# The last mixer of a gated attention and gMLP kernel, in pairs of row tiles with seven block products for eight

## The chip, the cores and the metric

The kernel runs on one core of a Trainium2 chip. The metric is the device time of one execution in microseconds (us). Three executions of the kernel before the change took 705.53, 705.56 and 706.84 us; their median is 705.56 us.

The engines are named as the profile names them: PE is the matrix engine (PEld its weight loads), DVE the Vector engine, ACT the Scalar engine, POOL GpSimd, SP the engine that issues most DMA transfers. PSUM is the memory that matmuls write, eight banks of 512 float32 columns for each of 128 partitions.

## The reference

One sequence of S = 2048 rows and D = 1024 columns goes through two branches, and a gate per row mixes them:

```python
g = _sigmoid((x * gate_w).sum(-1, keepdims=True))
a = _A_ref(x, A_wqkv, A_wo)          # attention over 8 positions, 2 apart, 32 heads of 32; then @ wo
b = _B_ref(x, B_w_in, B_w_sp, B_b_sp, B_w_out)
return g * a + (1 - g) * b
```

and the second branch is

```python
z = _gelu(jnp.einsum('bsd,df->bsf', x, w_in))        # f = 2 * 1792
z1 = z[..., :Fh].copy()
z2 = _layernorm(z[..., Fh:], axis=-1)
g = jnp.einsum('ts,bsf->btf', w_sp, z2) + b_sp[None, :, None]
return jnp.einsum('bsf,fd->bsd', z1 * g, w_out)      # u = z1 * g, 2048 x 1792, times w_out, 1792 x 1024
```

The last line is what this document calls the mixer: u times `w_out`.

## The kernel before

The rows are cut into 16 row tiles of 128, the 1792 features into 14 tiles of 128. Stages follow each other on PE: the gates' and `z2`'s matmuls, the queries, keys and values, `z1`, then the spatial product and the mixer, in four chunks of four row tiles (512 rows). Attention itself runs on DVE beside the first stages and leaves its output in DRAM (`o_d`), from where `load_oT` brings it back transposed, one row tile at a time.

Chunks 0 and 1 of the spatial product are plain (`g_chunk`): each of the 14 feature tiles sums 16 products. Chunks 2 and 3 together are done by `seven_products(n)`, called seven times, each for the feature tiles n and n + 7: the product of a 2x2 block matrix with a 2x2 block matrix, in seven block products of eight matmuls where eight block products would be plain. The sums of blocks that this takes (`s_sum` for `z2`, `t_sums` for `w_sp`) are made on DVE in float16; to keep float16 in range the rows of `w_sp` are scaled up by powers of two beforehand (`scale_rows`) and `omg` (1 - g) for rows 8 to 15 is scaled back down (`row_powers_back`). Partial sums that serve two results are copied on ACT from one PSUM bank to another, and matmuls go on adding there. `g_out` adds the bias and multiplies by `z1`, which an SP transfer has put in place; the result u lies in the first half of the `z2` tile of the feature before (`u_late`). While step n runs, DVE makes the sums of step n + 1.

`final_chunk(c)` then finishes four row tiles. For each half of 512 columns, `attn_mm` multiplies the attention output by `wo` (8 matmuls), `mixer_mm` multiplies u by `w_out` (14 matmuls), and `combine` scales the one by g on ACT, then the other by 1 - g on DVE, adding both; a transfer stores the row. The last row tile is cut into 512, 384 and 128 columns. The order is chunk 0, chunk 1, the seven steps, chunk 2, chunk 3.

Every engine runs its instructions in the order of the program text; nothing reorders them (`manual_schedule`). Work put off to a later moment goes through `beat`: `beat.at(t, f)` calls f once the matmuls written so far add up to time t, so that its instructions come at that point of the order. PSUM tiles come from one pool of eight banks in turn. SP's transfers are issued in program order as well, each when its own waits are over.

Of the kernel before, what the change touches and what calls it, by code (L numbers as in the profile page):

```python
# [27 lines left out]
FH = 1792  # L28
NF = FH // P
# [26 lines left out]
def kernel(  # L56
# [24 lines left out]
    def reg(off, n):  # L81
        return arena[:, off:off + n]
# [5 lines left out]
    o_d = dpool.tile([S, D], BF, name="o_d")  # L88
# [3 lines left out]
    ones = nc.const_aps.tensor(1.0, [P, 512], BF)  # L92
# [6 lines left out]
    ident = sm.tile([P, P], BF, name="ident")  # L99
# [36 lines left out]
    z2 = reg(Z_OFF, 16 * FH).rearrange("p (f i q) -> p f i q", f=NF, i=16)  # L136
    xT = reg(X_OFF, KT * S).rearrange("p (k s) -> p k s", k=KT)
    xT_flat = reg(X_OFF, KT * S)
    w_out_sb = reg(X_OFF, NF * D).rearrange("p (f n) -> p f n", f=NF)
# [23 lines left out]
    abs_out = reg(CD_OFF + 18944, 512)  # L163
# [3 lines left out]
    def half16(off, n):  # L167
        return reg(off, n * 512).bitcast(F16).rearrange("p (k t) -> p k t", k=n)
# [3 lines left out]
    u_first = reg(EF_OFF + 10240, 2048).rearrange("p (h i q) -> p h i q", h=2, i=8)  # L172
    t1 = half16(CD_OFF + 8192, 8)
    t2 = half16(A_OFF + 16384, 8)
    t3 = half16(EF_OFF, 8)
    t4_parts = [half16(X_OFF + NF * D, 4), half16(CD_OFF + 12288, 4)]

    x_v = x2.rearrange("(i q) d -> q i d", q=P)
    wq_v = A_wqkv.rearrange("(k p) c -> p k c", p=P)
# [5 lines left out]
    sync = nc.sync  # L185
# [38 lines left out]
    beat = Beat()  # L224
# [72 lines left out]
    TT = nc.vector.tensor_tensor  # L297
# [101 lines left out]
    def load_oT(a):  # L399
        sync.dma_start_transpose(oT_slots[a % 3], o_d[a * P:(a + 1) * P, :])  # L400
# [72 lines left out]
    for ch in range(NCH):  # L473
# [35 lines left out]
    for f in range(NF):  # L509
# [121 lines left out]
    def s_sum(n, k):  # L631
        a11, a12 = z2[:, n, 0:8, :], z2[:, n, 8:16, :]
        a21, a22 = z2[:, n + 7, 0:8, :], z2[:, n + 7, 8:16, :]
        if k == 0:
            TT(sums[0], a21, a22, ALU.add)
        elif k == 1:
            TT(sums[1], sums[0], a11, ALU.subtract)
        elif k == 2:
            TT(sums[2], a11, a21, ALU.subtract)
        else:  # L640
            TT(sums[3], a12, sums[1], ALU.subtract)

    def bank():
        return psum.tile([P, 512], F32, name="ps", tag="ps")

    def product(dst, lhs, rhs, first):
        for k in range(8):
            nc.tensor.matmul(dst[:], lhs[:, k, :], rhs(k), start=first and k == 0, stop=k == 7, skip_group_check=not first)  # L648

    def g_out(f, c, gsb):  # L650
        TT(gsb, gsb, bsp_bc[:, 512 * c:512 * (c + 1)], ALU.add)
        dst = u_late(f)[:, 4 * (c - 2):4 * (c - 1), :]
        TT(dst, gsb.rearrange("p (a q) -> p a q", a=4), dst, ALU.mult)

    def next_gsb():
        gs[0] += 1
        return gsb_slots[gs[0] % 3]

    def seven_products(n):
        fa, fb = n, n + 7  # L660
        for f in (fa, fb):
            sync.dma_start(u_late(f).rearrange("p (c a) q -> p c (a q)", c=2),
                           z1_d[2:4, :, f * 512:(f + 1) * 512].rearrange("c p t -> p c t"))
        more = n + 1 < 7
        e5 = asb_slots[n % 2]
        pa = bank()
        product(pa, z2[:, fa, 0:8, :], lambda k: b_lo[:, k], True)
        pb = bank()
        nc.scalar.copy(pb[:], pa[:])
        pe = bank()  # L670
        product(pe, sums[0], lambda k: t1[:, k], True)
        nc.scalar.copy(e5, pe[:])
        if more:
            s_sum(n + 1, 0)
        product(pb, sums[1], lambda k: t2[:, k], False)
        pc = bank()
        nc.scalar.copy(pc[:], pb[:])
        product(pa, z2[:, fa, 8:16, :], lambda k: b_lo[:, 8 + k], False)
        gsb = next_gsb()
        nc.scalar.copy(gsb, pa[:])  # L680
        g_out(fa, 2, gsb)
        product(pb, sums[2], lambda k: t3[:, k], False)
        gsb = next_gsb()
        TT(gsb, pb[:], e5, ALU.add)
        g_out(fb, 3, gsb)
        product(pc, sums[3], lambda k: b_hi[:, 8 + k], False)
        if more:
            s_sum(n + 1, 2)
        gsb = next_gsb()
        TT(gsb, pc[:], e5, ALU.add)  # L690
        g_out(fa, 3, gsb)
        product(pb, z2[:, fb, 8:16, :], lambda k: t4_parts[k // 4][:, k % 4], False)
        if more:
            s_sum(n + 1, 1)
            s_sum(n + 1, 3)
        gsb = next_gsb()
        nc.scalar.copy(gsb, pb[:])
        g_out(fb, 2, gsb)
        beat.run(56 * 512)

    def scaled_rows():
        t = beat.now
        natural(1)
        natural(2)
        for r in range(3):
            row_sums_fast(r)
        row_powers(0, 3, 1)
        row_powers_back()
        for r in range(4):
            load_wsp(3, r)  # L710
        for r in range(3):
            beat.at(t + 2.5 + 2.5 * r, lambda r=r: scale_rows(r))
        beat.at(t + 9.0, scaled_biases)
        for k, r in enumerate((3, 0, 1, 2)):
            beat.at(t + 8.0 + 3.5 * k, lambda r=r: load_wsp(2, r))

    def final_chunk(c):
        first = {}
        if c == 0:
            for a in range(3):  # L720
                for n0 in (0, 512):
                    first[a, n0] = mixer_mm(a, n0, 512)
            beat.flush(1e9)
            scaled_rows()
        if c == 1:
            for k in range(5):
                beat.at(beat.now + 12.0 + 3.0 * k, lambda k=k: t_sums(k))
            for k in range(2):
                beat.at(beat.now + 28.0 + k, lambda k=k: s_sum(0, k))
        for a in range(4 * c, 4 * c + 4):  # L730
            ob = ob_slots[a % 3]
            if a > 0 and a + 2 < 16:
                load_oT(a + 2)
            last = a == 15
            for part, (n0, nw) in enumerate(((0, 512), (512, 384), (896, 128)) if last else ((0, 512), (512, 512))):
                psa = attn_mm(a, n0, nw)
                psb = first[a, n0] if (a, n0) in first else mixer_mm(a, n0, nw)
                combine(a, n0, nw, part % 2, psa, psb)
                if last:
                    sync.dma_start(out2[a * P:(a + 1) * P, n0:n0 + nw], ob[:, n0:n0 + nw])  # L740
            if not last:
                sync.dma_start(out2[a * P:(a + 1) * P, :], ob)
# [14 lines left out]
    beat.at(t_rows + 40.0, lambda: natural(0))  # L757
    g_chunk(1)
    final_chunk(0)
    final_chunk(1)  # L760
    beat.flush(1e9)
    for k in (2, 3):
        s_sum(0, k)
    for n in range(7):
        seven_products(n)
    final_chunk(2)
    final_chunk(3)


# [28 lines left out]
```

## Time and profile before

The profiled execution took 706.58 us, of which the profile's span is 704.8 us; the median of the three timed executions is 705.56 us.

| stage | from, us | length, us | PE busy, us | DVE busy, us | ACT busy, us |
|---|---|---|---|---|---|
| `final_chunk(0)` | 463.0 | 39.8 | 38.30 | 14.84 | 11.68 |
| `final_chunk(1)` | 502.8 | 38.0 | 37.79 | 15.98 | 5.50 |
| seven steps | 540.8 | 84.6 | 84.23 | 48.98 | 19.70 |
| `final_chunk(2)` and `(3)` | 625.4 | 76.2 | 75.85 | 12.79 | 11.84 |
| whole execution | 0 | 704.8 | 696.2 | 458.3 | 279.1 |

In the lines of the profile, L561 is line 561 of the kernel. A group of instructions is given as line, engine, operation, output and input by name and shape, count, then busy time and mean duration in ns, then the engine's idle time just before them and what ended it. A line of the timeline starts with the time at which the instruction began and its duration. A window's columns are its ends and length, then busy time and count for PE, PEld, DVE, ACT and POOL, the granted PE clock, the DMA engines' busy share and GB/s. The chain that ended last is followed back from the last instruction, at each step to what released it.

### The profile page before, as it was taken

The numbers are of one execution on the slowest core, as the hardware profiler recorded it, in microseconds if no ns is written. First come the engines' busy times: TensorE is split into PE (matmuls) and PEld (weight loads), VectorE is DVE, ScalarE is ACT, GpSimd is POOL, SyncE is SP. The second block draws the span as 40 slices with busy tenths as digits, with TensorE's granted clock in tenths as the row PEclk, the third lists the DMA queues.
The fourth block names the chain that finished last, engine by engine and source line by source line (L and its number), as shares of the span: only waits on it lengthen the run. The fifth ranks groups of instructions, "written<-read, shape, count | busy, mean of one in ns | idle before, by whom it ended". The sixth has DMA issues, their size and how long they took to land.

```text
span 704.8 us, 8427 instructions
## 1 busy us (share of the span) xinstructions
PE 696.2 (99%) x3270; PEld 359.6 (51%) x3319; DVE 458.3 (65%) x496; ACT 279.1 (40%) x508; POOL 14.0 (2%) x23
## 2 busy tenths in 40 slices
PE   9999999999999999999999999999999999999998
PEld 4466666666665554444444444444444444444444
DVE  0000498999999999999999999852263565631111
ACT  4444544435369887344341229524211222221111
POOL 1000000000000211000000000000000000000000
PEclk9999999999999999999999999999999999999999
DMA  8994974976564122995249972299933111202210
GB/s 224 179 198 92 260 182 123 226 183 168 143 177 151 57 101 51 204 306 168 90 153 237 383 234 79 94 288 231 204 94 86 52 49 41 46 0 60 60 45 31
DMA packets 182967, 101.29 MB, mean 144 GB/s; under 512 B 145808, under 2 KB 171408, under 8 KB 182672
## 3 DMA queue, kind: packets, MB, share of 16 engines
q1 hardware_dynamic: 180624, 92.37, 50.1%
q10 hardware_dynamic: 2304, 8.39, 3.3%
q8 instruction: 26, 0.43, 0.2%
q14 instruction: 13, 0.11, 0.1%
HBM read 51.91 MB, written 32.57 MB: 120 GB/s over the span
## 4 chain that ended last, share of the span: by engine, by line
PE 97%; DMA 1%; issue 0%; SPq 0%; DVE 0%; DVEq 0%
PE ps L481 24%; PE ps L532 14%; PE psb L561 14%; PE ps L518 14%; PE ps L259 13%; PE ps L648 12%; PE psa L545 7%; DMA arena<-in_B_w_in_dram 1%; DMA arena<-o_d 1%; SPq L439 0%; SPq L437 0%; SPq L441 0%; DVE arena L569 0%; PE pt L584 0%; DVEq L569 0%
## 5 line engine op out<-in xcount | busy, mean ns | idle before, releaser
L481 PE MATMUL ps<-arena 128*128 128x512 bf16 x768 | 165.9, 379 | 0.0
L481 PEld LDWEIGHTS <-arena 128*128 128x128 bf16 x768 | 110.7, 144 | 55.1 <-issue 0.2
L303 DVE TENSOR_TENSOR arena<-arena 128x8192 bf16<-128x8192 bf16 x16 | 70.8, 4423 | 51.1 <-DMA arena<-k_d 50.9
L561 PE MATMUL psb<-arena 128*128 128x512 bf16 (+2 forms) x453 | 100.7, 372 | 0.5
L259 PE MATMUL ps<-arena 128*128 128x512 bf16 (+1 forms) x501 | 97.6, 353 | 1.3 <-DMA arena<-in_B_w_in_dram 0.6
L532 PE MATMUL ps<-arena 128*128 128x512 bf16 x439 | 96.6, 379 | 0.5
L518 PE MATMUL ps<-arena 128*128 128x512 bf16 x439 | 96.4, 379 | 0.5
L484 ACT CAST arena<-ps 128x512 bf16<-128x512 f32 x96 | 55.8, 587 | 93.2 <-PE ps L481 88.7
L569 DVE SCALAR_TENSOR_TENSOR arena<-psb,omg,arena 128x512 bf16<-128x512 f32 (+2 forms) x33 | 24.1, 734 | 104.9 <-PE psb L561 80.2
L648 PE MATMUL ps<-arena 128*128 128x512 f16 (+1 forms) x385 | 84.4, 379 | 0.4
L306 DVE TENSOR_TENSOR arena<-arena 128x4096 bf16<-128x4096 bf16 (+1 forms) x64 | 77.5, 1211 | 1.9
L259 PEld LDWEIGHTS <-arena 128*128 128x128 bf16 x512 | 50.2, 98 | 48.4 <-issue 1.9
L561 PEld LDWEIGHTS <-arena 128*128 128x128 bf16 x462 | 44.6, 98 | 52.1
L336 DVE TENSOR_TENSOR arena<-arena,att_A 128x8192 bf16<-128x8192 bf16 x16 | 70.7, 4421 | 0.2
L518 PEld LDWEIGHTS <-arena 128*128 128x128 bf16 x448 | 43.8, 98 | 52.7
L532 PEld LDWEIGHTS <-arena 128*128 128x128 bf16 x448 | 43.8, 98 | 52.6
L568 ACT ACTIVATE arena<-psa,g_s 128x512 f32<-128x512 f32 (+2 forms) x33 | 22.1, 674 | 121.9 <-PE psa L545 116.4
L648 PEld LDWEIGHTS <-arena 128*128 128x128 bf16 (+1 forms) x392 | 38.3, 98 | 46.3
L545 PE MATMUL psa<-arena 128*128 128x512 bf16 (+2 forms) x260 | 59.5, 372 | 1.6 <-DMA arena<-o_d 1.3
L520 ACT ACTIVATE arena<-ps 128x512 bf16<-128x512 f32 x56 | 32.2, 597 | 51.5 <-PE ps L518 39.1
L264 ACT ACTIVATE arena<-ps 128x512 bf16<-128x512 f32 (+1 forms) x64 | 34.3, 539 | 25.5 <-PE ps L259 25.3
L545 PEld LDWEIGHTS <-arena 128*128 128x128 bf16 x264 | 25.5, 98 | 31.2 <-DMA arena<-o_d 1.5
(93 smaller groups left out, 399.7 us busy)
## 6 DMA issues: line engine op xcount, KB each, us to landing
arena<-k_d SPq DMA_DIRECT2D x8, 960.0 KB, 7.3
arena<-v_d SPq DMA_DIRECT2D x8, 960.0 KB, 5.4
z_d<-arena SPq DMA_DIRECT2D x14, 512.0 KB, 4.0
arena<-in_A_wqkv_dram SPq DMA_DIRECT2D x24, 256.0 KB, 4.5
arena<-in_B_w_in_dram SPq DMA_DIRECT2D x4, 1024.0 KB, 6.6
q_d<-arena SPq DMA_DIRECT2D x32, 128.0 KB, 2.3
k_d<-arena SPq DMA_DIRECT2D x32, 128.0 KB, 2.3
v_d<-arena SPq DMA_DIRECT2D x32, 128.0 KB, 2.5
```

What stands on the lines that cost most here:

```text
L259: nc.tensor.matmul(ps[:, 0:N], xT[:, kt, i * P:(i + 1) * P], w2[:, kt, ZC * c:ZC * c + N], start=(kt == 0), stop=(kt == KT - 1))
L264: nc.scalar.activation(z2[:, 4 * c:4 * c + n // P, i, :], ps[:, 0:n].rearrange("p (f q) -> p f q", q=P), ACT.Gelu_apprx_tanh, accum_out=s1 ...
L303: TT(prod.rearrange("p (w j c) -> p w j c", w=W, j=8, c=C), in0, in1, ALU.mult)
L306: return lambda: TT(pv[:, :, 0:half], pv[:, :, 0:half], pv[:, :, half:2 * half], ALU.add)
L336: TT(prod.rearrange("p (w j d h) -> p w j d h", w=W, j=8, d=DH, h=HG), in0, in1, ALU.mult)
L481: nc.tensor.matmul(ps[:].rearrange("p (t c) -> p t c", t=4), lhsT, wgt[:, :, kt, :], start=(kt == 0), stop=(kt == KT - 1))
L484: nc.scalar.copy(st[:, j % 4, :], ps[:])
L518: nc.tensor.matmul(ps[:], w1[:, kt, (f % 4) * P:(f % 4 + 1) * P], xT[:, kt, 512 * c:512 * (c + 1)], start=(kt == 0), stop=(kt == KT - 1))
L532: nc.tensor.matmul(ps[:], z2[:, f, i, :], wsp[:, i, :, :].rearrange("p a t -> p (a t)"), start=(i == 0), stop=(i == 15))
L545: nc.tensor.matmul(psa[:, 0:nw], oT_slots[a % 3][:, kt, :], wo_sb[:, kt, n0:n0 + nw], start=(kt == 0), stop=(kt == KT - 1))
L561: nc.tensor.matmul(psb[:, 0:nw], u_tile(f, a), w_out_sb[:, f, n0:n0 + nw], start=(f == 0), stop=(f == NF - 1))
L648: nc.tensor.matmul(dst[:], lhs[:, k, :], rhs(k), start=first and k == 0, stop=k == 7, skip_group_check=not first)
```

## The change

The mixer of row tiles 8 to 15 (chunks 2 and 3) is no longer `mixer_mm`. Row tiles are taken in four pairs, the 14 feature tiles in two halves of seven and `w_out` in two halves of columns, so that u of a pair is a 2x2 block matrix and `w_out` another; `late_mix` multiplies them with the same scheme as the seven steps, seven block products of seven matmuls each. The attention's products stay as they are, 16 matmuls per row tile.

- `w_largest` (four reductions over `w_out`) and `whole_power` find one power of two for `w_out`; `whole_power` takes the largest of 128 partitions by a transpose on PE, a reduction on DVE and a matmul with ones that spreads it again, and multiplies `omg` by what scales back. Both are placed in `final_chunk(1)` through `beat`.
- In step n of the seven, for n of 1 and more, `w_scale(n - 1)` scales two tiles of `w_out` in place and `w_sum` makes four float16 sums of its halves, in the second halves of the `z2` tiles that the step before has used. `u_sums(n - 1)` on ACT adds up absolute values of u, from which `whole_power` later takes the power for u.
- After the seven steps, `late_chunks` does the attention products of row tiles 8 to 11 (`attn_pair`, `attn_half`) with the last tile's weights, the power for u and the first pair's sums (`prepare`: `u_scale`, then four `u_sum`) beside them; then pair 0, the attention products of row tiles 12 and 13, pairs 1, 2 and 3, and last the attention products of 14 and 15, with the last row tile cut as before. `prepare(q + 1)` stands after the sixth product of pair q.
- In the pairs ACT copies partial sums between banks and DVE combines; for the last pair ACT also scales the mixer's part.
- The transposed loads of row tiles 10 to 15 (`late_oT`) move: 10 ahead of the seven steps, 11 to 14 to their end, 15 once row 8's attention product frees its place. Two copies on ACT bring `u_first` into `z2`.

The diff, cut to its core:

```diff
@@ seven_products
         gsb = next_gsb()
         nc.scalar.copy(gsb, pa[:])
+        if n:
+            u_sums(n - 1)
         g_out(fa, 2, gsb)
+        if n:
+            w_scale(n - 1)
         product(pb, sums[2], lambda k: t3[:, k], False)
...
         g_out(fb, 3, gsb)
+        if n:
+            w_sum(n - 1, 0)
+            w_sum(n - 1, 1)
         product(pc, sums[3], lambda k: b_hi[:, 8 + k], False)
...
         g_out(fa, 3, gsb)
+        if n:
+            w_sum(n - 1, 2)
+            w_sum(n - 1, 3)
         product(pb, z2[:, fb, 8:16, :], lambda k: t4_parts[k // 4][:, k % 4], False)
...
+    def whole_power(src, up1):
+        v = nc.vector
+        v.tensor_scalar(top[:], src, TINY, None, ALU.max)
...
+        v.tensor_copy(top_b[:], top_i[:].bitcast(F32))
+        yield
+        po = psum.tile([P, 512], F32, name="po", tag="ps")
+        pt = po[0:1, 0:P // 2].bitcast(BF)
+        nc.tensor.transpose(pt, top_b[:], ident[:])
+        v.tensor_reduce(top_1[:], pt, AX.X, ALU.max)
+        yield
+        nc.tensor.matmul(po[:], ones[0:1, 0:P], top_1[:].to_broadcast([1, 512]), start=True, stop=True)
+        v.tensor_copy(top[:], po[:, 0:1])
...
+        v.tensor_scalar(omg[:, 8:16], omg[:, 8:16], back[:].bitcast(F32), None, ALU.mult)
+        yield
...
+    def w_scale(j):
+        for f in ((j + 1) % 7, (j + 1) % 7 + 7):
+            nc.vector.tensor_scalar(w_out_sb[:, f, :], w_out_sb[:, f, :], w_up[:].bitcast(F32), None, ALU.mult)
...
+    def u_scale(q):
+        v = z2[:, :, 2 * q:2 * q + 2, :]
+        nc.vector.tensor_scalar(v, v, u_up[:].bitcast(F32), None, ALU.mult)
...
+    def late_mix(q, done, added, ready):
+        s = late_sums[q % 2]
+        a, b = 8 + 2 * q, 9 + 2 * q
+        e5 = late_e5[q % 2]
+        pa = bank()
+        product7(pa, lambda j: z2[:, j, 2 * q, :], lambda j: w_tiles(j)[0], True)
+        pb = bank()
+        nc.scalar.copy(pb[:], pa[:])
+        pe = bank()
+        product7(pe, lambda j: s[0][:, j, :], lambda j: w_t(j, 0), True)
+        added(pe, e5)
+        product7(pb, lambda j: s[1][:, j, :], lambda j: w_t(j, 1), False)
+        pc = bank()
+        nc.scalar.copy(pc[:], pb[:])
+        product7(pa, lambda j: z2[:, 7 + j, 2 * q, :], lambda j: w_tiles(j)[2], False)
+        done(a, 0, pa)
+        product7(pb, lambda j: s[2][:, j, :], lambda j: w_t(j, 2), False)
+        done(b, 512, pb)
+        product7(pc, lambda j: s[3][:, j, :], lambda j: w_tiles(j)[3], False)
+        done(a, 512, pc)
+        ready()
+        product7(pb, lambda j: z2[:, 7 + j, 2 * q + 1, :], lambda j: w_t(j, 3), False)
+        done(b, 0, pb)
...
+        u_sums(6)
+        nc.vector.tensor_reduce(top[:], u_l1[:], AX.X, ALU.max)
+        steps = whole_power(top[:], u_up)
+        next(steps)
+        w_scale(6)
+        for k in range(4):
+            w_sum(6, k)
+        attn_pair(0)
+        next(steps)
+        attn_half(10, 0)
+        next(steps)
+        prepare(0)
+        for a, n0 in ((10, 512), (11, 0), (11, 512)):
+            attn_half(a, n0)
+        for a in (12, 13, 14, 15):
+            sync.dma_start_transpose(late_oT[a], o_d[a * P:(a + 1) * P, :])
+        pair(0)
+        attn_pair(2)
+        pair(1)
+        pair(2)
+        last_pair(3)
@@ final_chunk, c == 1
+            for k in range(4):
+                beat.at(beat.now + 0.5 + 2.5 * k, lambda k=k: w_largest(k))
+            w_steps = whole_power(top[:], w_up)
+            for k in range(3):
+                beat.at(beat.now + 26.0 + 4.0 * k, lambda: next(w_steps))
@@ the end
+    sync.dma_start_transpose(late_oT[10], o_d[10 * P:11 * P, :])
     for n in range(7):
         seven_products(n)
-    final_chunk(2)
-    final_chunk(3)
+        if n == 5:
+            nc.scalar.copy(z2[:, 13, 0:8, :], u_first[:, 1])
+    nc.scalar.copy(z2[:, 6, 0:8, :], u_first[:, 0])
+    sync.dma_start_transpose(late_oT[11], o_d[11 * P:12 * P, :])
+    late_chunks()
```

More of the change, by code (lines that the diff above doesn't have):

```diff
@@ L128 @@
     b_up = sm.tile([P, 8], BF, name="b_up")
+    w_max = sm.tile([P, 4], F32, name="w_max")
+    u_l1 = sm.tile([P, 28], F32, name="u_l1")
+    top = sm.tile([P, 1], F32, name="top")
+    top_i = sm.tile([P, 1], I32, name="top_i")
+    top_b = sm.tile([P, 1], BF, name="top_b")
+    top_1 = sm.tile([1, 1], BF, name="top_1")
+    w_up = sm.tile([P, 1], I32, name="w_up")
+    u_up = sm.tile([P, 1], I32, name="u_up")
+    back = sm.tile([P, 1], I32, name="back")
     att_L = sm.tile([P, 2 * W * 8 * HG], F32, name="att_L")
@@ L176 @@
     t4_parts = [half16(X_OFF + NF * D, 4), half16(CD_OFF + 12288, 4)]
+    w_sums = reg(Z_OFF, 16 * FH).bitcast(F16).rearrange("p (f i n) -> p f i n", f=NF, i=4)
+    late_asb = [reg(CD_OFF + r * 1024, 1024).bitcast(F32) for r in range(8)]
+    late_oT = {a: oT_slots[a % 3] for a in (8, 9, 10)}
+    for r, a in enumerate((11, 12, 13, 14)):
+        late_oT[a] = reg(CD_OFF + 8192 + r * 1024, 1024).rearrange("p (k t) -> p k t", k=KT)
+    late_oT[15] = late_oT[8]
+    late_ob = ob_slots + [reg(A_OFF + 14336, 1024)]
+    late_e5 = [reg(A_OFF + 16384 + r * 1024, 1024).bitcast(F32) for r in range(2)]
+    late_sums = [[reg(EF_OFF + (4 * r + k) * 896, 896).bitcast(F16).rearrange("p (k q) -> p k q", k=7)
+                  for k in range(4)] for r in range(2)]
     x_v = x2.rearrange("(i q) d -> q i d", q=P)
@@ L699, in seven_products @@
         beat.run(56 * 512)
+    def whole_power(src, up1):
+        v = nc.vector
+        v.tensor_scalar(top[:], src, TINY, None, ALU.max)
+        v.tensor_scalar(top_i[:], top[:].bitcast(I32), 23, None, ALU.logical_shift_right)
+        v.tensor_scalar(top_i[:], top_i[:], 23, None, ALU.logical_shift_left)
+        v.tensor_copy(top_b[:], top_i[:].bitcast(F32))
[7 more added lines that the diff above has]
+        v.tensor_copy(top[:], po[:, 0:1])
+        v.tensor_scalar(top_i[:], top[:].bitcast(I32), 23, None, ALU.logical_shift_right)
+        v.tensor_scalar(up1[:], top_i[:], -1, 254 + TOP, ALU.mult, ALU.add)
+        v.tensor_scalar(up1[:], up1[:], 23, None, ALU.logical_shift_left)
+        v.tensor_scalar(back[:], top_i[:], -TOP, None, ALU.add)
+        v.tensor_scalar(back[:], back[:], 23, None, ALU.logical_shift_left)
+        v.tensor_scalar(omg[:, 8:16], omg[:, 8:16], back[:].bitcast(F32), None, ALU.mult)
+        yield
@@ new lines, in w_largest, with w_tiles @@
+    def w_largest(k):
+        f0, f1 = (0, 4, 8, 11, 14)[k:k + 2]
+        nc.vector.tensor_reduce(w_max[:, k:k + 1], w_out_sb[:, f0:f1, :].rearrange("p f n -> p (f n)"), AX.X, ALU.max,
+                                apply_absolute_value=True)
+        if k == 3:
+            nc.vector.tensor_reduce(top[:], w_max[:], AX.X, ALU.max)
+    def w_tiles(j):
+        f = (j + 1) % 7
+        return (w_out_sb[:, f, 0:512], w_out_sb[:, f, 512:1024],
+                w_out_sb[:, f + 7, 0:512], w_out_sb[:, f + 7, 512:1024])
@@ new lines, in w_t, with w_sum @@
+    def w_t(j, k):
+        return w_sums[:, j + 7 * (k // 2), 2 + k % 2, :]
+    def w_scale(j):
+        for f in ((j + 1) % 7, (j + 1) % 7 + 7):
+            nc.vector.tensor_scalar(w_out_sb[:, f, :], w_out_sb[:, f, :], w_up[:].bitcast(F32), None, ALU.mult)
+    def w_sum(j, k):
+        b11, b12, b21, b22 = w_tiles(j)
+        if k == 0:
+            TT(w_t(j, 0), b12, b11, ALU.subtract)
+        elif k == 1:
+            TT(w_t(j, 1), b22, w_t(j, 0), ALU.subtract)
+        elif k == 2:
+            TT(w_t(j, 2), b22, b12, ALU.subtract)
+        else:
+            TT(w_t(j, 3), b21, w_t(j, 1), ALU.subtract)
@@ new lines, in u_sums, with u_sum @@
+    def u_sums(n):
+        for h, f in enumerate((n, n + 7)):
+            for k in range(2):
+                c = 4 * n + 2 * h + k
+                nc.scalar.activation(abs_out.rearrange("p (i q) -> p i q", i=4), u_late(f)[:, 4 * k:4 * k + 4, :], ACT.Abs,
+                                     accum_out=u_l1[:, c:c + 1])
+    def u_scale(q):
+        v = z2[:, :, 2 * q:2 * q + 2, :]
+        nc.vector.tensor_scalar(v, v, u_up[:].bitcast(F32), None, ALU.mult)
+    def u_sum(q, k):
+        s = late_sums[q % 2]
+        a11, a12 = z2[:, 0:7, 2 * q, :], z2[:, 7:14, 2 * q, :]
+        a21, a22 = z2[:, 0:7, 2 * q + 1, :], z2[:, 7:14, 2 * q + 1, :]
+        if k == 0:
+            TT(s[0], a21, a22, ALU.add)
+        elif k == 1:
+            TT(s[1], s[0], a11, ALU.subtract)
+        elif k == 2:
+            TT(s[2], a11, a21, ALU.subtract)
+        else:
+            TT(s[3], a12, s[1], ALU.subtract)
@@ new lines, in late_attn, with late_slot, attn_half @@
+    def late_attn(a, n0, nw=512):
+        psa = psum.tile([P, 512], F32, name="psa", tag="ps")
+        for kt in range(KT):
+            nc.tensor.matmul(psa[:, 0:nw], late_oT[a][:, kt, :], wo_sb[:, kt, n0:n0 + nw],
+                             start=(kt == 0), stop=(kt == KT - 1))
+        return psa
+    def late_slot(a, n0):
+        return late_asb[2 * (a % 4) + n0 // 512]
+    def attn_half(a, n0):
+        psa = late_attn(a, n0)
+        nc.scalar.activation(late_slot(a, n0), psa[:], ACT.Copy, scale=g_s[:, a:a + 1])
@@ new lines, in attn_pair, with product7 @@
+    def attn_pair(q):
+        for a in (8 + 2 * q, 9 + 2 * q):
+            for n0 in (0, 512):
+                attn_half(a, n0)
+    def product7(dst, lhs, rhs, first):
+        for j in range(7):
+            nc.tensor.matmul(dst[:], lhs(j), rhs(j), start=first and j == 0, stop=j == 6, skip_group_check=not first)
+    def late_mix(q, done, added, ready):
+        s = late_sums[q % 2]
+        a, b = 8 + 2 * q, 9 + 2 * q
[19 more added lines that the diff above has]
+        done(b, 0, pb)
@@ new lines, in late_chunks, with prepare, out_row, pair @@
+    def late_chunks():
+        stt = nc.vector.scalar_tensor_tensor
+        def prepare(q):
+            u_scale(q)
+            for k in range(4):
+                u_sum(q, k)
+        def out_row(a):
+            sync.dma_start(out2[a * P:(a + 1) * P, :], late_ob[a % 4])
+        def pair(q):
+            a, b = 8 + 2 * q, 9 + 2 * q
+            def added(pe, e5):
+                nc.scalar.copy(e5, pe[:])
+                for r in (b, a):
+                    stt(late_slot(r, 512), e5, omg[:, r:r + 1], late_slot(r, 512), ALU.mult, ALU.add)
+            def done(r, n0, ps):
+                stt(late_ob[r % 4][:, n0:n0 + 512], ps[:], omg[:, r:r + 1], late_slot(r, n0), ALU.mult, ALU.add)
+                if (r, n0) in ((a, 512), (b, 0)):
+                    out_row(r)
+            late_mix(q, done, added, lambda: prepare(q + 1))
+        def last_pair(q):
+            a, b = 8 + 2 * q, 9 + 2 * q
+            def added(pe, e5):
+                for r in (b, a):
+                    nc.scalar.activation(late_slot(r, 512), pe[:], ACT.Copy, scale=omg[:, r:r + 1])
+            def done(r, n0, ps):
+                if n0:
+                    stt(late_slot(r, n0), ps[:], omg[:, r:r + 1], late_slot(r, n0), ALU.mult, ALU.add)
+                else:
+                    nc.scalar.activation(late_slot(r, n0), ps[:], ACT.Copy, scale=omg[:, r:r + 1])
+            late_mix(q, done, added, lambda: None)
+            for r in (a, b):
+                ob = late_ob[r % 4]
+                parts = ((0, 512), (512, 512)) if r == a else ((0, 512), (512, 384), (896, 128))
+                for n0, nw in parts:
+                    psa = late_attn(r, n0, nw)
+                    mix = late_slot(r, 512 * (n0 // 512))[:, n0 % 512:n0 % 512 + nw]
+                    stt(ob[:, n0:n0 + nw], psa[:, 0:nw], g_s[:, r:r + 1], mix, ALU.mult, ALU.add)
+                    if r == b:
+                        sync.dma_start(out2[r * P:(r + 1) * P, n0:n0 + nw], ob[:, n0:n0 + nw])
+                if r == a:
+                    out_row(r)
+        u_sums(6)
[11 more added lines that the diff above has]
+        for a, n0 in ((10, 512), (11, 0), (11, 512)):
+            attn_half(a, n0)
+        for a in (12, 13, 14, 15):
[5 more added lines that the diff above has]
+        last_pair(3)
@@ L729, in final_chunk @@
                 beat.at(beat.now + 28.0 + k, lambda k=k: s_sum(0, k))
+            for k in range(4):
+                beat.at(beat.now + 0.5 + 2.5 * k, lambda k=k: w_largest(k))
+            w_steps = whole_power(top[:], w_up)
+            for k in range(3):
+                beat.at(beat.now + 26.0 + 4.0 * k, lambda: next(w_steps))
         for a in range(4 * c, 4 * c + 4):
```

## The prediction

> **What bounds the kernel now.** I read the page first (busy shares, chain that ended last), then the stages as windows, then the timeline of one step of the stage before the change.
>
> ```profile
> PE 696.2 (99%) x3270; PEld 359.6 (51%) x3319; DVE 458.3 (65%) x496; ACT 279.1 (40%) x508; POOL 14.0 (2%) x23
> ...
> PE 97%; DMA 1%; issue 0%; SPq 0%; DVE 0%; DVEq 0%
> ```
>
> ```profile
> 502.80:540.80 38.00, 37.79 (x174) 17.22 (x177) 15.98 (x15) 5.50 (x8) 0.00 (x0) 1.00 0.45 101
> 540.80:625.40 84.60, 84.23 (x387) 38.33 (x393) 48.98 (x95) 19.70 (x34) 0.00 (x0) 1.00 0.18 50
> 625.40:701.60 76.20, 75.85 (x369) 35.65 (x373) 12.79 (x19) 11.84 (x18) 0.00 (x0) 1.00 0.17 44
> ```
>
> TensorE is the path from end to end, at granted clock 1.00 in every stage: a matmul removed is time saved as long as nothing it waits for becomes late. The three windows are `final_chunk(1)`, the seven `seven_products` steps, and chunks 2 and 3 (columns: length, PE, weight loads, DVE, ACT, POOL, clock, DMA share, GB/s). DVE is at 42%, 58% and 17% there. The new work falls on it, so the reader should look at how tightly it sits inside one step:
>
> ```profile
> 596.84 0.42 DVE L651 TENSOR_TENSOR arena<-arena 128x512 bf16<-128x512 bf16 x1 [3.38 <-ACT arena L680]
> 597.30 0.42 DVE L653 TENSOR_TENSOR arena<-arena 128x512 bf16<-128x512 bf16 x1
> 597.95 0.69 DVE L684 TENSOR_TENSOR arena<-ps,arena 128x512 bf16<-128x512 f32 x1 [0.23 <-PE ps L648]
> 598.67 0.42 DVE L651 TENSOR_TENSOR arena<-arena 128x512 bf16<-128x512 bf16 x1
> 599.13 0.42 DVE L653 TENSOR_TENSOR arena<-arena 128x512 bf16<-128x512 bf16 x1
> 599.48 0.68 DVE L639 TENSOR_TENSOR arena<-arena 128x1024 f16<-128x1024 bf16 x1
> 600.08 0.68 DVE L690 TENSOR_TENSOR arena<-ps,arena 128x512 bf16<-128x512 f32 x1
> 600.80 0.43 DVE L651 TENSOR_TENSOR arena<-arena 128x512 bf16<-128x512 bf16 x1
> 601.26 0.43 DVE L653 TENSOR_TENSOR arena<-arena 128x512 bf16<-128x512 bf16 x1
> 601.60 0.68 DVE L637 TENSOR_TENSOR arena<-arena 128x1024 f16<-128x1024 f16 x1
> ```
>
> Two spacings to see: an instruction that needs the result before it starts 0.03 us after its end (0.46 after a 0.42 start); one that doesn't starts 0.08 before that end (599.13 to 599.48 is 0.35). Durations of the new kinds of work are taken from:
>
> ```profile
> L414 DVE TENSOR_SCALAR arena<-arena,mean,rstd 128x1792 bf16<-128x1792 bf16 x16 | 10.9, 742 | 1.8 <-POOL rstd L410 1.8
> L580 DVE TENSOR_REDUCE l<-arena 128x1 f32<-128x2048 bf16 x3 | 6.8, 2282 | 4.3 <-DMA arena<-in_B_w_sp_dram 4.3
> ```
>
> **The change, part by part.** Line numbers beside new functions are the changed kernel's, all others this profile's. *Matmuls removed.* The seven steps start at 540.77 and end at 625.38: 84.61/392 = 0.2158 us a matmul. The mixer of eight rows falls from 8 x 28 = 224 to 4 x 7 x 7 = 196: -28 x 0.2158 = **-6.04**. float16 costs nothing extra here, since steps already mix f16 and bf16 at this rate. Added: two transposes of 128 columns (0.056, from 14 matmuls of 128 columns in 0.94 - 0.22) and two of 512 (0.216): **+0.54**.
>
> *`w_largest` and the first `whole_power`, in `final_chunk(1)`.* Four reductions, two of 4096 (2 x 2.24) and two of 3072 (3.36): 15.7 us on DVE, which goes from 16 to 32 of 38. Queued behind them are the combines (L569), so ACT's copies, PSUM banks, row stores and, behind those on SP, `load_oT`. The worst combine, of row 4's second half, slips from 512.5 to 520.0; its bank is wanted four halves (19 us) later, and row 7's transposed load is issued near 521, lands by 527 and is needed at 531.27. Covered. TensorE itself waits at the transpose (L740), behind row 7's first attention half, at 531.27 + 1.73 = 533.0. DVE gets there from 503.06 by six combines (0.67 start to start), the reductions (8.74 + 6.6), three t sums (2.2), two (1.15) and five small ones (1.0): 4.0 + 15.3 + 6.6 + 2.3 + 1.0 = 29.3, so 532.4. 0.6 to spare: **0** (0 to 1.2).
>
> *`w_scale`, `w_sum`, `u_sums` in the steps.* A step starting at 589.17 has its seventh product at 599.53; it waits for L684's read of the bank. The next step's third product is due at 604.71 and loads the sums of L637. Into that chain go two `w_scale` and four `w_sum` of 0.425 (L653's row). `w_scale` has no row; between a share of L414 (0.42) and all of L414 (0.74) I take the line through L414 and a 16-element TENSOR_SCALAR (0.175): 0.50, as in form it is L414's kind. Then: scales at 597.65 and 598.07; L684's successor 598.49 to 599.18, in time for 599.53; add and multiply to 600.0; two sums, one needing the other, 0.81; s sum 0.60; L690's successor 0.72; add, multiply 0.81; two sums 0.70; L637's successor ends at 604.34 against 602.28. With 0.10 from DVE to its waiter (L538 ends 422.81, ACT starts 422.91) that is 604.44 against 604.71. **0** (at 0.74: 604.82 and 599.66, some 0.23 late in six steps, 1.4).
> On ACT, four `u_sums` of 0.755 (spacing of the L577 pairs) are 3.0 in the 4.59 idle ahead of L697. The copy of `u_first` (1.1, half of L614's 2000 ns; at worst L248's 2.0) sits ahead of L669, whose result is due 1.5 us after L669 starts in a free step: at worst level. The z1 loads on SP now wait for L637's successor, 3.2 us into the step instead of 1.9; landing 3.5 later (at most 5.0) they make 6.7 (8.2) against 8.1. In step 0, row 10's transposed load ahead of them adds 1.3: 543.6 + 5.0 = 548.6, needed 548.9.
>
> *Handover to the pairs.* ACT: copy until 627.2, four `u_sums` to 630.2; DVE: five small operations of 0.2, 631.25; TensorE reaches the transpose after four attention halves, 625.38 + 6.91 = 632.3. DVE then does scales and sums of the last pair of weights before its reduction of the transposed maxima: 634.0. TensorE has one half to cover it, to 634.1: **0** (0 to 0.5). The next seven small operations, `u_scale(0)` and its sums end near 639.4; the first pair starts at 639.5 and needs only the scale (637.1), and its second product, 1.5 later, the first sum (637.7). The five moved `load_oT` (1.3 each to issue, 4.7 to land) go out from 617 on with no store before 650: covered.
>
> *Between pairs 1, 2 and 3 nothing covers the scale.* `prepare(q+1)` stands behind the combine of product six, and the next pair's first weight load needs `u_scale`. Product seven lasts 7 x 0.2158 = 1.51. From its start: combine at 0.27 (630.40 against 630.13), next start 0.67 later, 0.94. `u_scale` (3584 elements) lies between 0.74 (one L414, half as wide) and 1.48 (two); the same line gives 1.31, nearest the upper end: 2.25, plus 0.10: 2.35 - 1.51 = 0.84, twice: **+1.7** (0.55 to 2.0). The sums come behind it: 0.62 each, due 1.5 apart. Pair 0 to 1 has four attention halves, 6.9. ACT's copies (0.57) start 0.2 into a 1.51 product and are due at its end.
> By the Trainium skill, "VectorE: DVE Perf Modes", section "Side-by-side: where the cycles go for N=2048 bf16", such a scale moves four elements a cycle plus some 158 cycles; estimates from the page are 0.43 and 1.10, the stalls would be 1.3 and the sum 0.4 lower.
>
> *End.* The last row ends with attention parts of 512, 384 and 128 columns. The 128 columns take 0.45, so L569's 0.62 then 0.35 end 0.5 after TensorE, against 0.47: **0**.
>
> Sum: -6.04 + 0.54 + 1.70 = -3.8. The profiled execution took 706.58 (span 704.8, 1.78 around it), 1.0 above the median 705.56; it would become 702.8, so the median **701.8**. A measurement of this kernel can tell about 0.2% (1.4 us): 704.15 and 706.97 are the marks.
>
> **The rivals.**
> *A. DVE limits the steps.* Both scales at L414's upper prices: 1.4 in the steps and 2.0 between pairs leave -6.04 + 0.54 + 3.4 + 0.1 = -2.0: **703.6**. For it: 0.27 to 0.35 us of slack. Against: it needs a scale of 1024 elements to cost what 1792 do.
> *B. Slower: the scales run one element at a time,* as L684's 512 in 0.69 do. `w_scale` is then 1.2; two add 1.4 ahead of L684's successor, which ends at 600.58, 1.15 late in each of six steps (6.9). `u_scale` is 3.9: 3.4 late, twice (6.9). -5.5 + 13.8 = +8: **714**. It turns to slower from a `w_scale` of about 0.85, with `u_scale` in proportion. Against: L414 is the same operation, in place, with scalars per partition, at 2.4 elements a ns.
> *C. Slower: no Vector instruction starts before the one ahead has ended.* Nine free starts in the chain at 0.11 each end it 1.0 later: 0.7 late in five steps (3.5) and 0.1 at six seventh products (0.5); 16 starts in `final_chunk(1)` leave TensorE 1.2 late; the pairs 0.96 each (1.9). -5.5 + 7.1 = +1.6: **707.2**. Against: 599.13 to 599.48.
> The Trainium skill, same page, "The DRAIN you can't avoid", states that rule for every operation, with an exception for one that isn't held; the rows above agree with the exception.
> That the change does not remove the matmuls can't be: 3281 stand in its program against 3319: 28 of the mixer gone, 14 that split the last row's mixer, and four added.
>
> **How the numbers follow.** Forecast 0.62 (700.6 to 702.9, by 0.55 to 2.0 of stalls with up to 0.8 of small ones); A 0.20, of it 0.16 faster and 0.04 same; B 0.07; C 0.05; unlisted 0.06 (0.04 same, 0.02 slower). Faster 0.78, same 0.08, slower 0.14. The range 700.6 to 704.2 holds forecast and most of A.
>
> **What would show it.** The `w_scale` rows near 0.50 and the third product (L668) with no idle before it; the pairs' first weight load (L828) twice idle for about 0.8 on `u_scale` (L792), which takes about 1.3; no idle at L740 and L743; the seven steps still 84.6 long, the late stage 72 instead of 76. Steps longer than 12.1 mean A; scale rows over 1 us mean B. A wait on DVE at L740, or on ACT's `u_sums` at the handover, would make the forecast too low.

## The result and the profile after

The changed kernel takes 702.32 us (median of six executions, 701.98 to 702.83) against 705.54 us for the kernel before (six executions): a ratio of 0.9953, 95% interval 0.994 to 0.9966, or 2.4 to 4.2 us less. The prediction was 701.8 us in a range of 700.6 to 704.2. The range held, and two of its terms were mis-sized in opposite directions; the sections below show both.

First the page of the changed kernel: busy time by engine, and the chain that ended last.

```profile
PE 694.3 (99%) x3281; PEld 356.0 (51%) x3281; DVE 510.4 (73%) x596; ACT 306.0 (44%) x576; POOL 14.0 (2%) x23
...
PE 98%; DMA 1%; DVE 1%; issue 0%; DVEq 0%
```

TensorE is still the path, but DVE has entered the chain with 1%. Where, the three stages tell. Here they are as windows, each cut at the start of its first matmul, the last at the end of TensorE's work; first the kernel before, then the changed one. Columns: ends and length, then busy time and count for PE, weight loads, DVE, ACT and POOL, the granted clock, DMA share, GB/s.

```profile
502.78:540.77 37.99, 37.78 (x173) 17.21 (x176) 15.98 (x15) 5.50 (x8) 0.00 (x0) 1.00 0.45 101
540.77:625.38 84.61, 84.24 (x387) 38.34 (x393) 48.96 (x95) 19.70 (x34) 0.00 (x0) 1.00 0.18 50
625.38:701.56 76.18, 75.86 (x369) 35.67 (x373) 12.81 (x19) 11.84 (x18) 0.00 (x0) 1.00 0.17 44
```

```profile
501.88:540.55 38.67, 38.67 (x180) 17.24 (x179) 32.65 (x32) 5.50 (x8) 0.00 (x0) 1.00 0.46 101
540.55:625.15 84.60, 84.60 (x393) 38.37 (x392) 59.63 (x127) 37.38 (x83) 0.00 (x0) 1.00 0.23 63
625.15:697.08 71.93, 71.14 (x335) 31.99 (x333) 37.46 (x70) 21.19 (x37) 0.00 (x0) 1.00 0.09 30
```

`final_chunk(1)` grew by 0.68, the seven steps by nothing although DVE has 10.7 us more to do in them, and the late stage lost 4.25. Together that is -3.57 us. The two profiled executions differ by more (706.58 and 702.09, 4.49): the missing 0.90 lies ahead of the first window, which begins at 502.78 in the one and at 501.88 in the other. Nothing that runs there was changed. The traces show where the 0.90 arises: the stage at line 481 (501 in the changed kernel) begins at 37.89 in the one and at 37.13 in the other, behind waits of 0.16 and 0.48 for the first loads of `w_in` that the changed kernel's trace does not have, and a wait for the attention's output at 492 took 1.34 and 1.20. In the seven experiments below, whose work up to there is that of the changed kernel, the first matmul of that window starts between 501.83 and 502.53. So nothing ties the 0.90 to the change, and the stages, not the spans, are compared in what follows.

The late stage, as TensorE's timeline of the changed kernel (start, duration, instruction, count, and in brackets idle time with what ended it):

```profile
632.15 0.22 PE L740 MATMUL po<-ident,top_b 128*1 128x128 bf16 x1
632.30 1.90 PE L810 MATMUL psa<-arena 128*128 128x512 bf16 x8
634.13 0.39 PE L743 MATMUL po<-top,const-bfloat16-1.0 1*128 1x512 bf16 x1
634.45 5.35 PE L810 MATMUL psa<-arena 128*128 128x512 bf16 x24
639.64 10.74 PE L828 MATMUL ps<-arena 128*128 128x512 bf16 x49
650.22 7.07 PE L810 MATMUL psa<-arena 128*128 128x512 bf16 x32
657.13 10.74 PE L828 MATMUL ps<-arena 128*128 128x512 bf16 x49
668.26 10.75 PE L828 MATMUL ps<-arena 128*128 128x512 bf16 x49 [0.40 <-DVE arena L792]
679.41 10.75 PE L828 MATMUL ps<-arena 128*128 128x512 bf16 x49 [0.40 <-DVE arena L792]
```

Read by starts, since ends are modelled. Pair 0 needs 650.22 - 639.64 = 10.58, which is 49 x 0.2158. Pair 1 to pair 2 takes 11.13 and pair 2 to pair 3 takes 11.15: 0.55 and 0.57 lost, 1.12 in all. (The bracket shows 0.40, because a matmul's modelled end reaches 0.16 beyond the next one's start.) The handover shows a loss that no bracket has: the 32 attention matmuls from 625.15 would be done at 632.06, and from there to 634.45 the 2.39 us hold 8 x 0.2158 = 1.73 of attention, so `whole_power` cost 0.66. Its columns are 0.27. The late stage adds up: -6.04 (28 matmuls) + 0.66 + 1.12 = -4.26, against -4.25 measured. `final_chunk(1)` has the other `whole_power` and grew by 0.68. So all of the result is in three terms.

### The profile page after: what moved, and what is told of

Its sections match the earlier page's. It is cut to its first block, busy times and chain, and to the rows that moved or that the text cites. A ratio compares the mean times of both kernels' runs of the same rounds, so it can differ in the third digit from the quotient of the medians.

```text
span 700.3 us, 8570 instructions
## 1 busy us (share of the span) xinstructions
PE 694.3 (99%) x3281; PEld 356.0 (51%) x3281; DVE 510.4 (73%) x596; ACT 306.0 (44%) x576; POOL 14.0 (2%) x23
## 4 chain that ended last, share of the span: by engine, by line
PE 98%; DMA 1%; DVE 1%; issue 0%; DVEq 0%
PE ps L501 24%; PE ps L279 14%; PE ps L552 14%; PE ps L538 14%; PE ps L668 12%; PE psb L581 7%; PE ps L828 6%; PE psa L810 4%; PE psa L565 3%; DMA arena<-o_d 1%; PE pw L97 0%; DVE arena L792 0%; PE pt L295 0%; DVE arena L874 0%; PE po L743 0%; DVE arena L900 0%
## 5 line engine op out<-in xcount | busy, mean ns | idle before, releaser
L501 PEld LDWEIGHTS <-arena 128*128 128x128 bf16 x768 | 110.7, 144 | 55.1
L279 PE MATMUL ps<-arena 128*128 128x512 bf16 (+1 forms) x512 | 98.0, 354 | 0.0
L504 ACT CAST arena<-ps 128x512 bf16<-128x512 f32 x96 | 55.7, 587 | 93.4 <-PE ps L501 88.9
L668 PE MATMUL ps<-arena 128*128 128x512 bf16 (+1 forms) x392 | 84.8, 379 | 0.0
L279 PEld LDWEIGHTS <-arena 128*128 128x128 bf16 x512 | 50.2, 98 | 47.5 <-issue 1.0
L538 PEld LDWEIGHTS <-arena 128*128 128x128 bf16 x448 | 43.9, 98 | 52.6
L552 PEld LDWEIGHTS <-arena 128*128 128x128 bf16 x448 | 43.8, 98 | 52.6
L581 PE MATMUL psb<-arena 128*128 128x512 bf16 x224 | 50.2, 379 | 0.0
L828 PE MATMUL ps<-arena 128*128 128x512 f16 (+1 forms) x196 | 43.0, 379 | 0.8 <-DVE arena L792 0.8
L556 ACT CAST arena<-ps 128x512 bf16<-128x512 f32 x28 | 16.3, 582 | 52.1 <-PE ps L552 26.9
L362 DVE TENSOR_TENSOR arena<-arena 128x4096 bf16<-128x4096 bf16 x16 | 36.6, 2290 | 0.4
L588 ACT ACTIVATE arena<-psa,g_s 128x512 f32<-128x512 f32 x16 | 10.9, 686 | 58.2 <-PE psa L565 47.0
L581 PEld LDWEIGHTS <-arena 128*128 128x128 bf16 x224 | 21.8, 98 | 26.2 <-issue 0.2
```

The source lines that it names most:

```text
L279: nc.tensor.matmul(ps[:, 0:N], xT[:, kt, i * P:(i + 1) * P], w2[:, kt, ZC * c:ZC * c + N], start=(kt == 0), stop=(kt == KT - 1))
L362: return [(4.4, mul), (2.3, lambda: TT(p3[:, 0:4, :], p3[:, 0:4, :], p3[:, 4:8, :], ALU.add)), (1.2, lambda: TT(p3[:, 0:2, :], p3[:, 0:2, ...
L504: nc.scalar.copy(st[:, j % 4, :], ps[:])
L552: nc.tensor.matmul(ps[:], z2[:, f, i, :], wsp[:, i, :, :].rearrange("p a t -> p (a t)"), start=(i == 0), stop=(i == 15))
L828: nc.tensor.matmul(dst[:], lhs(j), rhs(j), start=first and j == 0, stop=j == 6, skip_group_check=not first)
```

## The experiments

All are the changed kernel with one edit, except the last, which has two. Line numbers in the lines of their profiles can be a few off those of the changed kernel. Only the first and the last were executed more than once; the others are compared by their stages. Stages that an edit leaves alone repeat to 0.01 us: `final_chunk(1)` took 38.66 to 38.67 in three of these runs, the seven steps 84.60 to 84.61 in five, the late stage 71.93 in two.

### Is `u_scale` all that the pairs wait for?

```diff
 def prepare(q):
-    u_scale(q)
+    if q < 2:
+        u_scale(q)
...
 pair(0)
+u_scale(2)
+u_scale(3)
 attn_pair(2)
```

> The changed kernel with u_scale of pairs 2 and 3 written right behind pair 0, beside the attention products of rows 12 and 13, and nothing else moved. In the changed kernel's trace the first matmul of a pair comes 10.58 us after that of the pair before plus 0.55 and 0.57 (657.13, 668.26, 679.41), and the late stage runs from 625.15 to 697.08, 71.93 us. Theory (u_scale alone is uncovered): the three pairs follow each other at 10.58, the late stage takes 70.8, 1.1 less, and nothing else takes the place of the wait, since the first sum is then ready 1.5 us before its product. Rival (the combine of product six and the sums behind it hold the next pair as well, and u_scale was only the last in line): 0.1 to 0.5 of idle stays at each of the two pairs, at the weight load of the first or second product, late stage 71.2 to 71.9.

The timeline of TensorE in this run, from pair 1 on:

```profile
657.22 31.89 PE L828 MATMUL ps<-arena 128*128 128x512 bf16 x145
```

The three pairs are one unbroken row (3 x 10.58 + 0.16 = 31.90; two records are missing from the count of 147). The late stage took 70.79 instead of 71.93, 1.14 less, as the theory said, and no other wait came in its place: the combine of product six and the sums were covered. In time it is 701.74 us (four executions), ratio to the kernel before 0.9937 (0.9921 to 0.9954), an interval that can't be told from the changed kernel's; the verdict rests on the trace.

### Why `whole_power` costs 0.67 and not 0.27

In the changed kernel's trace there are about 0.1 us ahead of and behind each of its matmuls, and DVE was done long before: the column of maxima at 630.74 for a transpose at 632.15, the reduced maximum at 633.17 for a matmul at 634.13. Three runs ask what the gaps hang on.

One: full rows for the spreading matmul. It has weights of 1 row and 128 columns; here 127 rows of zeros are added to the operand.

```diff
-top_1 = sm.tile([1, 1], BF, name="top_1")
+top_1 = sm.tile([P, 1], BF, name="top_1")
+nc.gpsimd.memset(top_1[:], 0.0)
...
-nc.tensor.matmul(po[:], ones[0:1, 0:P], top_1[:].to_broadcast([1, 512]), ...)
+nc.tensor.matmul(po[:], ones[:, 0:P], top_1[:].to_broadcast([P, 512]), ...)
```

> The changed kernel with the spreading matmul over 128 rows instead of one (127 of them zero), so that its weights are 128x128; the transpose ahead of it is as it was. Theory (only weights that don't fill the array break the loading ahead): the gaps before and behind the spreading matmul, 0.10 each, go; final_chunk(1) 38.47 instead of 38.67, late stage 71.73 instead of 71.93; those around the transpose stay. Rival (a lone matmul breaks it whatever its shape): 38.67 and 71.93.

```profile
632.16 0.22 PE L741 MATMUL po<-ident,top_b 128*1 128x128 bf16 x1
632.31 1.90 PE L811 MATMUL psa<-arena 128*128 128x512 bf16 x7
634.05 0.38 PE L744 MATMUL po<-top,const-bfloat16-1.0 128*128 128x512 bf16 x1
634.26 2.97 PE L811 MATMUL psa<-arena 128*128 128x512 bf16 x13
```

Eight matmuls from 632.31 (one record is missing) end at 634.04, so the gap ahead is 0.01 where it was 0.10, and 0.21 to the next is the matmul's own 512 columns. The transpose, untouched, keeps its 0.15 to the next, of which 0.056 are its columns. `final_chunk(1)` took 38.45 and the late stage 71.71: 0.22 less each.

Two: fewer columns instead.

```diff
-nc.tensor.matmul(po[:], ones[0:1, 0:P], top_1[:].to_broadcast([1, 512]), ...)
+nc.tensor.matmul(po[:, 0:8], ones[0:1, 0:P], top_1[:].to_broadcast([1, 8]), ...)
```

> The changed kernel with the spreading matmul of whole_power cut from 512 columns to 8 (only one is read). From its start to the next matmul's takes 0.32 us in the changed kernel, and its own columns account for 0.216. Theory (gaps of a fixed size around it, plus its columns): 0.11 to 0.15 to the next matmul, final_chunk(1) 38.5 instead of 38.67, late stage 71.75 instead of 71.93. Rival (the time to the next matmul is that of emptying the array and loading anew, in which the columns are hidden): 0.3 stays, 38.67 and 71.93.

```profile
634.00 0.17 PE L743 MATMUL po<-top,const-bfloat16-1.0 1*128 1x8 bf16 x1
634.10 3.19 PE L810 MATMUL psa<-arena 128*128 128x512 bf16 x14
```

The time to the next matmul falls from 0.32 to 0.10, just under the 0.11 to 0.15 expected: the 504 columns saved are worth 0.21 each time (38.46 and 71.72), and 0.10 remains that no column accounts for. The gap is thus a fixed cost added to the columns; it does not hide them. The output of this variant is wrong (by 0.31, relative), and why stays open; only its times are read here.

Three: one matmul with full weights in place of both. The column of maxima repeated 128 times as weights, against the identity, puts all 128 maxima on every partition, and one reduction ends it.

```diff
-nc.tensor.transpose(pt, top_b[:], ident[:])
-v.tensor_reduce(top_1[:], pt, AX.X, ALU.max)
-yield
-nc.tensor.matmul(po[:], ones[0:1, 0:P], top_1[:].to_broadcast([1, 512]), ...)
-v.tensor_copy(top[:], po[:, 0:1])
+nc.tensor.matmul(po[:, 0:P], top_b[:].to_broadcast([P, P]), ident[:], ...)
+v.tensor_reduce(top[:], po[:, 0:P], AX.X, ALU.max)
+yield
```

> whole_power with one matmul in place of the transpose and the spreading matmul: the column of 128 maxima, repeated 128 times, as weights of 128x128 against the identity, and one reduction of 128x128 on DVE. In the changed kernel each whole_power lengthens PE's path by 0.67 us, of which only 0.27 is the time of its columns; the rest lies in four gaps of about 0.1, ahead of and behind each of the two matmuls. Theory (weights that fill only one column or one row of the array are not loaded while other matmuls run, nor the full ones behind them): full weights load ahead, each whole_power costs 0.06 to 0.10, final_chunk(1) falls from 38.67 to 38.1 and the late stage from 71.93 to 71.35. Rival (any lone matmul in the stream, or a wait on DVE, costs these gaps, whatever its weights): 0.25 each, 38.25 and 71.5.

Here with the weight loads (PEld), in order of time:

```profile
631.51 0.10 PEld L739 LDWEIGHTS <-top_b 128*128 128x128 bf16 x1
...
631.72 0.22 PE L739 MATMUL po<-ident,top_b 128*128 128x128 bf16 x1
...
631.78 5.56 PE L807 MATMUL psa<-arena 128*128 128x512 bf16 x24
```

The load now starts 0.21 ahead of its matmul, beside the attention's last, and the next matmul follows after 0.06. In the changed kernel the load of the 128x1 weights was recorded at 632.15, the same moment as its matmul (shown above), and so was the load behind it at 632.30:

```profile
632.15 0.08 PEld L740 LDWEIGHTS <-top_b 128*1 128x1 bf16 x1 [0.42 <-DVE arena L775]
...
632.30 1.41 PEld L810 LDWEIGHTS <-arena 128*128 128x128 bf16 x8
```

(The releaser named there had nothing to do with it: the weights were ready at 630.74, and with full weights the wait is gone.) `final_chunk(1)` took 38.04 and the late stage 71.30, 0.63 less each, which is what the theory gave (38.1 and 71.35) and the rival didn't (38.25 and 71.5). That run also has a lone matmul of 128 columns that takes its weights from DVE, so neither of these makes the gap. What all three show: weights of one row or one column were not loaded while other matmuls ran, nor were the full weights behind them, at 0.09 to 0.10 a time.

The third run also replaces a transpose by a plain matmul. But being a transpose does not keep a load back: of the 16 transposes with 128x128 weights at the start of the changed kernel (`L295`), the last has its load at 5.06 and starts at 5.17, and the plain matmul behind it has its load at 5.17 and starts at 5.27.

No run tried a size between one and 128, but the trace of the kernel before has one, the first transpose of the biases, with weights of 8 rows, in the middle of a full stream:

```profile
407.67 7.07 PE L532 MATMUL ps<-arena 128*128 128x512 bf16 x32
414.67 0.17 PE L584 MATMUL pt<-ident,b_row 8*128 8x8 bf16 x1
414.78 7.51 PE L532 MATMUL ps<-arena 128*128 128x512 bf16 x33
```

The 32 matmuls end at 407.67 + 32 x 0.2158 = 414.58. That leaves 0.09 ahead of it, and 0.11 to the next, of which its 8 columns are under 0.01: the same two gaps.

### How much room DVE has in the steps

The steps kept their 84.60 us. To see how near the edge they are, Vector work was added right where `w_scale` stands: one tile multiplied once more by one, then (without the condition on f) both.

```diff
 for f in ((j + 1) % 7, (j + 1) % 7 + 7):
     nc.vector.tensor_scalar(w_out_sb[:, f, :], ..., w_up[:].bitcast(F32), None, ALU.mult)
+    if j < 6 and f < 7:
+        nc.vector.tensor_scalar(w_out_sb[:, f, :], ..., unit[:], None, ALU.mult)
```

> The changed kernel with one Vector instruction more in each of steps 1 to 6: a tile of w_out (1024 elements) multiplied once more, by one, right behind the two scales; 0.40 us from start to start, as the second of the two scales. In the changed kernel's trace the seventh product of a step is due 0.42 us after DVE has read its bank, and the third product of the next step 0.48 after its sum is ready, less 0.05 from DVE to its waiter: about 0.4 us free in each step. Theory (DVE has just this room): the six steps grow by 0 to 0.05 each, the steps together 84.6 to 84.9. Rival A of the prediction in a sharper form (DVE already sets the end of the steps, and the trace hides it): six times 0.4, 87.0. Rival D (DVE has far more room than the two waits show, since other products can go ahead): 84.6 here and also with two.

> The same with both tiles multiplied once more by one, 0.80 us of Vector work more in each of steps 1 to 6, as if each scale took 0.88. Theory (room of about 0.4): the seventh product waits 0.35 to 0.45 in six steps, the third product of the next step then nothing more; the steps take 86.7 to 87.3 instead of 84.6. Rival A sharpened: 89.4. Rival D: 84.6. If both products wait one after the other, 6 x 0.8 = 89.4 as well, told from rival A by the run with one scale more.

The steps took 85.90 with one (541.20 to 627.10) and 89.01 with two (540.65 to 629.66): 1.30 and 4.41 more, 0.22 and 0.74 in each of six steps. I had expected 0 to 0.05 and 0.35 to 0.45. DVE's timeline of the first run shows what was wrong:

```profile
598.71 0.48 DVE L772 TENSOR_SCALAR arena<-arena,w_up 128x1024 bf16<-128x1024 bf16 x1
599.23 0.49 DVE L774 TENSOR_SCALAR arena<-arena,unit 128x1024 bf16<-128x1024 bf16 x1
599.63 0.48 DVE L772 TENSOR_SCALAR arena<-arena,w_up 128x1024 bf16<-128x1024 bf16 x1
600.03 0.68 DVE L710 TENSOR_TENSOR arena<-ps,arena 128x512 bf16<-128x512 f32 x1
```

The second multiplication reads what the first wrote, so it starts 0.52 after it, while the next scale, of another tile, starts 0.40 after that. From the first scale to the read of the bank (`L710`, the sum of `pb` and `e5`) it is 1.32 instead of 0.79 in the changed kernel: 0.53 added, not 0.40. With two it is 1.83, 1.04 added. Take the same room off both: 0.53 - 0.31 = 0.22, and 1.04 - 0.31 = 0.73. Two runs, one number: DVE has 0.31 us to spare in each step, and past it every 0.1 costs 0.1, six times. The changed kernel's own trace has that number too: DVE has read the bank at 598.89 (598.21 + 0.68), and the seventh product is due at 599.25 (540.55 + 4 x 12.086 + 48 x 0.2158), 0.36 later, less 0.05 to its waiter. The 0.42 of my expectation does not come out of that trace. The wait is where the prediction looked for it: in the run with two, TensorE stands idle at the seventh product of each of the six steps for the read of its bank. One of them:

```profile
589.47 12.25 PE L670 MATMUL ps<-arena 128*128 128x512 f16 x56 [0.58 <-DVE arena L710]
```

So both rivals fall: DVE does not set the end of the steps yet (that would be 6 x 0.53 = 3.2 for one), and it does not have much room either.

### Both edits together

> Both of the edits that took time off TensorE's path: the scales of pairs 2 and 3 beside the attention products of rows 12 and 13, and one matmul with full weights in whole_power. If they are independent, final_chunk(1) takes 38.05, the seven steps 84.6 and the late stage 71.93 - 1.14 - 0.63 = 70.16 us, 2.4 less in all than the changed kernel: a median of 699.9 beside 702.3, a ratio to the kernel before of 0.992. If the shorter handover uncovers u_scale(0) and its sums (their last ended 0.4 us ahead of the first pair's start in the changed kernel, and the first sum is due 1.5 us after it), the late stage would be up to 0.3 longer.

```profile
501.83:539.88 38.05, 38.05 (x179) 17.31 (x178) 32.41 (x31) 5.50 (x8) 0.00 (x0) 1.00 0.51 106
539.88:624.48 84.60, 84.60 (x393) 38.34 (x392) 59.60 (x127) 37.40 (x83) 0.00 (x0) 1.00 0.25 63
624.48:694.65 70.17, 70.17 (x334) 32.20 (x332) 37.12 (x69) 21.20 (x37) 0.00 (x0) 1.00 0.09 31
```

38.05, 84.60 and 70.17: the edits are independent, 2.38 us less than the changed kernel by the stages, and in the last stage TensorE has no idle time left. The median of six executions is 700.41 us (699.65 to 702.68), where 699.9 was expected; the ratio to the kernel before is 0.993 (0.9919 to 0.9942), beside 0.9953 for the changed kernel. Of the kernels timed in several executions this one has the lowest median.

## Why the prediction was right, point by point

*Matmuls removed, -6.04.* Right. Pair 0 takes 49 x 0.2158, float16 and bfloat16 mixed, and the late stage adds up with 28 matmuls less to 0.01 us.

*Added matmuls, "+0.54".* This term was mis-sized: 0.66 + 0.68 = 1.34. I priced the transposes and the spreading matmuls by their columns. The trace of before had a price, and I took none from it: `L584`, shown above, loses 0.09 ahead of it and 0.11 behind. Four matmuls at 0.2 each on top of the 0.54 make 1.34. The four gaps of 0.1 in each `whole_power` stand where a weight load is recorded at the moment of its own matmul instead of ahead of it.

*`w_largest` and the transpose in `final_chunk(1)`, 0.* Right. The reductions took 8.74 and 6.60 as worked out, and the column of maxima was ready at 531.08, for a transpose at 532.19: 1.0 to spare before the gap, 0.6 predicted.

*The steps, 0.* Right, and by about the margin given. `w_scale` took 0.479 (0.50 estimated), the sums 0.42, and the room that the runs found, 0.31, lies in the 0.27 to 0.35 of the working. Of its two waits the seventh product's bank is the nearer. The case of a 0.74 scale can be checked too: 2 x (0.74 - 0.479) = 0.52 more, which is the added time of the first of the two runs, and costs 0.22 in each of six steps where the prediction said 0.23.

*The handover, 0.* TensorE waited for nothing there: the reduced maximum came 0.9 ahead of its matmul. But the loss of 0.39 beyond the columns lies just at these two places, "no idle at L740 and L743" was said of them, and only the list of waits would have agreed.

*Between pairs, "+1.7".* The mechanism was right, down to the two places and to `u_scale` as what ends the wait; the size was too large: 1.12. Pair 1 to 2 by its terms, from the start of product seven (657.13 + 42 x 0.2158 = 666.19):

```profile
666.39 0.75 DVE L874 SCALAR_TENSOR_TENSOR arena<-ps,omg,arena 128x512 bf16<-128x512 f32 x1 [0.76 <-PE ps L828]
667.06 1.15 DVE L792 TENSOR_SCALAR arena<-arena,u_up 128x3584 bf16<-128x3584 bf16 x1
...
668.26 10.75 PE L828 MATMUL ps<-arena 128*128 128x512 bf16 x49 [0.40 <-DVE arena L792]
```

The combine starts after 0.20 (0.27 predicted), `u_scale` 0.67 later (as predicted), takes 1.15 (1.31), and TensorE starts 0.05 after its end (0.10): 2.07 - 1.51 = 0.56 instead of 0.84. The largest share is the scale's own duration. My line ran through the row of before with 1792 elements in 742 ns, which takes two scalars (`mean` and `rstd`); through the two new rows, 1024 elements in 479 and 3584 in 1146 ns, 1792 would be at 679. The Trainium skill's estimates, from "VectorE: DVE Perf Modes", section "Side-by-side: where the cycles go for N=2048 bf16", were 0.43 and 1.10. Both rows are 0.05 above them; for `u_scale` the page was nearer than my line, for `w_scale` my line was.

*End, 0.* Right: the last combine ends 0.48 after TensorE, 0.47 before.

*The sum.* -3.8 predicted, -3.57 by the stages, -3.2 by the medians. 0.8 too little at the added matmuls and 0.6 too much between the pairs nearly cancel; the forecast's last microsecond is luck. Of the rivals, none came: A had 1.4 in the steps and 2.0 between the pairs, where nothing and 1.12 were measured; the scales run 3.8 elements to the nanosecond (2560 more elements in 667 ns), so the slower rival by scales of one element at a time is out; independent instructions on DVE start 0.08 before the one ahead ends (599.63 + 0.48 against 600.03), so the rival without overlap is out as well, while the dependent pair above shows what it would have been. The Trainium skill's page, section "The DRAIN you can't avoid", says that the next instruction waits until the pipe of the one ahead is empty, and that one which isn't held starts earlier. The rows agree: 0.52 from start to start for the one that reads what the one ahead wrote, 0.40 for one that doesn't.

## What to carry to other kernels

In this TensorE-bound kernel a block scheme that saves matmuls paid its whole count wherever its extra Vector work stood beside other matmuls. Look for the places between two rounds where the preparation of the next round is written behind the last result of this one, and move the part that needs only old data up to where Vector is idle. Matmuls with weights of one row, one column or eight rows in a full stream cost 0.2 us here beyond their columns; 128x128 weights, by repeating a column or adding rows of zeros, took that off where it was tried. And a stage that keeps its length under more Vector work says nothing on how near the edge it is; adding a bit of work twice measures the room, if what it adds is read from the trace.

## What the runs showed that was not expected

Weights of 128x1 or 1x128 broke the loading ahead on both sides, 0.09 to 0.10 us each, and the profile puts no wait on TensorE's matmuls there; the rows of the weight loads have idle time (0.42 at `L740`), but only the starts tell what is lost. An instruction in place on what the one ahead wrote cost 0.12 more on DVE than one on another tile (0.52 against 0.40). Two things stay open. The variant with a spreading matmul of 8 columns gave a wrong output, and its cause is open. And in every trace TensorE waits 1.1 to 1.6 us at 492 to 493 for a transfer of the attention's output, in the kernel before (1.34) as after; no run here was made for it.
